# V products on 32-row groups of the array, two at a time, with U, V and the low-rank values held twice

## The chip, the cores and the metric

The kernel is one program on one NeuronCore of a Trainium2 chip. The metric is device time in microseconds (us) for one launch, and smaller is better. Three timed runs of the kernel before gave 225.97, 226.92 and 228.09 us; their median is 226.92. A separate execution was recorded by the hardware profiler, and every row of the trace quoted below is from that one. Its own device time is 224.48 us, and its span, from the first to the last instruction, is 222.7 us.

Engines are named as in the profile: PE is the matrix engine, PEld its weight loads, DVE the vector engine, ACT the scalar engine, POOL GpSimd, SP the engine whose queue issues most of the DMAs.

## What is computed

An attention layer and a mixer, both in one launch. The reference, cut to what matters:

```python
# attention: q, k, v are (4 batches, 8 heads, 768 positions, 64)
scores = q @ k.T / sqrt(64) - slope[h] * distance
scores = where(first 8 keys or the last 96 positions, scores, -1e9)
attn = softmax(scores) @ v
x = attn, heads side by side: (4, 768, 512)

# mixer: U is (768, 32), V is (32, 768), w_ch1 (512, 2048), w_ch2 (2048, 512)
h = x.T @ U @ V                       # over the positions, rank 32
u = x + h.T
out = u + relu(u @ w_ch1) @ w_ch2
```

The change touches only `h`: the product with U, which leaves 32 low-rank values per channel, and the product of these with V.

## The kernel before, in words

**Tiling.** Positions are cut into 6 blocks of 128, the 512 channels into 4 blocks of 128, which are 2 heads each. A *pair* `i` is one batch's two heads: 16 pairs, 4 per batch. Operands are fp16, sums are fp32 in the eight banks of PSUM, each 512 fp32 wide.

**A pair's steps.** Scores by matmuls with a contraction of 64, where the two heads stand on rows 0 to 63 and 64 to 127 of the array and write to different banks. In the first batch they are `st_sc` (L323, added to a bias from a matmul with all 128 rows, L316). In the other batches they are `visit` (L359): 22 matmuls in one block, 11 for each head, alternating. Then the exponential on ACT (L343 in the first batch; in the others L378, after L370 on DVE), the product with the values (`st_av`, L389 and L393), the normalisation on DVE (L406, L413), a cast to fp16 on POOL (L417).

**The low-rank part of a pair.** `st_up` (L423) for the first five pairs that need the result at once, or `st_low` (L431), its copy `st_lc` (L437, DVE) and a transpose `st_lt` (L441, PE) for the other eleven, gives the low-rank values of 128 channels. They stand on 32 partitions of PSUM, the other 96 hold zeros, because U is held in a tile 128 columns wide of which 32 are not zero. `st_tc` (L446, DVE) copies all 128 partitions to `tmp`. The product with V follows, and all of it contracts over 128 partitions of which 96 hold zeros:

- `st_M2` (L481, L486), first batch, 4 pairs: for each half of the positions one V product of 384 columns, then three matmuls that add the transposed attention into the same bank. The sum goes to `uT` by `st_ut` (ACT or DVE).
- `st_M3` (L454), other batches, 12 pairs: six V products of 128 columns, three into one bank and three into another; `st_add` (L464, L471) adds them to `x` on DVE, and a DMA transposes the sum into `uT`.
- `down_mm` (L542), first batch only: one V product of 512 columns opens the accumulation for each of the 6 blocks of output positions.

**The feed-forward part.** `up_mm` (L527) is one step `U(b, g, jt)` of four matmuls; `up_relu` (L535, ACT) takes its bank. `down_mm` (L547) has four parts of four matmuls for each block of positions in the first two batches. In the last two batches `product` (L614) takes its place, with sums on DVE (L601, L632).

**What sets the order.** The order on every engine is written by a planner inside the kernel (from L642). Every step has a planned cost, dependencies, and a count of banks; the planner keeps a clock for each engine and emits the next step that can start, and a bank is granted when the step that reads it last has its planned end. So a planned cost that changes moves steps of all engines against each other. Before 30 us of its clock it fills planned idle time of PE with `warm` matmuls (L152), whose result nothing reads. What is emitted is a fixed order; on the chip each engine runs its own queue in that order and waits by semaphores.

Of the kernel before, what the change touches and what calls it, by code (L numbers as in the profile page):

```python
# [20 lines left out]
def kernel(  # L21
# [13 lines left out]
    nc = tc.nc  # L35
# [3 lines left out]
    P = 128  # L39
# [5 lines left out]
    R = moe_U.shape[1]  # L45
# [16 lines left out]
    GT = S // 2  # L62
    NTG = GT // P
# [15 lines left out]
    banks = [psum.tile([P, 512], FP32, name=f"bank{j}") for j in range(8)]  # L79
    granted = deque()  # L80

    def bank(dtype=FP32):
        t = granted.popleft()
        return t if dtype == FP32 else t.bitcast(dtype)
# [97 lines left out]
    v16w = cst.tile([P, S], FP16, name="v16w")  # L182
    for t in (u16.rearrange("p n c -> p (n c)"), v16w):
        nc.gpsimd.memset(t.bitcast(I32), 0)
    nc.gpsimd.dma_start(u16[:, :, 0:R], moe_U.rearrange("(c p) r -> p c r", p=P))
    nc.gpsimd.dma_start(v16w[0:R], moe_V)
    ident16 = cst.tile([P, P], FP16, name="ident16")
    nc.vector.tensor_copy(ident16, ident)

# [244 lines left out]
            )  # L434

    def st_lc(i):
        nc.vector.tensor_copy(lows[i % 2][:, 0:R], tms[i][:, 0:R])  # L437

    def st_lt(i):
        back = tms[i].bitcast(FP16)[:, 4 * P:5 * P]  # L440
# [7 lines left out]
    def st_M3(i):  # L448
        b, dc = i // NP, i % NP
        for g in range(2):  # L450
            ups = bank()
            for t in range(NTG):
                n = NTG * g + t
                nc.tensor.matmul(  # L454
                    ups[:, t * P:(t + 1) * P], v16w[:, n * P:(n + 1) * P],
                    tmps[b][:, dc * P:(dc + 1) * P],
                    start=(t == 0), stop=(t == NTG - 1),
                )
            ups3[i, g] = ups

    def st_add(i, g):
        b, dc = i // NP, i % NP
# [13 lines left out]
    def st_M2(i):  # L476
        b, dc = i // NP, i % NP
        ch = slice(dc * P, (dc + 1) * P)
        for g in range(2):
            ups = bank()  # L480
            nc.tensor.matmul(  # L481
                ups[:, 0:GT], tmps[b][:, ch], v16w[:, g * GT:(g + 1) * GT],
                start=True, stop=False,
            )
            for t in range(NTG):
                nc.tensor.matmul(  # L486
                    ups[:, t * P:(t + 1) * P], x16s[b][:, dc, NTG * g + t], ident16,
                    start=False, stop=(t == NTG - 1),
                )
            ups3[i, g] = ups  # L490

    def st_ut(i, g, eng):
        b, dc = i // NP, i % NP
# [43 lines left out]
    def down_mm(b, n, part):  # L537
        g, ts = group(b, n)
        if part == 0:
            cps_t[b, n] = bank()  # L540
            if b == 0:
                nc.tensor.matmul(  # L542
                    cps_t[b, n], v16w[:, n * P:(n + 1) * P], tmps[0], start=True, stop=False,
                )
        cps, htr = cps_t[b, n], htrs[b, g]
        for jc in range(4 * part, 4 * part + 4):
            nc.tensor.matmul(  # L547
                cps, htr[:, jc, ts], w2_16[:, jc],
                start=(b > 0 and jc == 0), stop=(jc == NJC - 1),
            )  # L550
# [264 lines left out]
    def first(i):  # L815
        if i:
            casts(i)
            turns(i)
        values(i)
        for c in range(3):  # L820
            sc = add(("sc", i, c), "PE", 0.85 if c < 2 else 0.7, lambda c=c: st_sc(i, c),
                     [], banks=2, at=0 if i or not c else 7.9,
                     soft=[(("tq", i), 0.4), (("tk", i), 0.4), (("ka", i), 0.6)])
            free_of[sc] = [
                add(("ex", i, c, hi), "ACT", 0.56 if c < 2 else 0.46,
                    lambda c=c, hi=hi: st_ex(i, c, hi), [("sc", i, c), ("av", i - 2, hi)])
                for hi in range(2)
            ]
        for hi in range(2):
            a = add(("av", i, hi), "PE", 0.33, lambda hi=hi: st_av(i, hi),  # L830
                    [("ex", i, c, hi) for c in range(3)] + [("va", i), ("vp", i)], banks=1)
            free_of[a] = [add(("n", i, hi), "DVE", 0.75, lambda hi=hi: st_norm(i, hi), [("av", i, hi)])]
            if i < NP - 1:
                add(("x16", i, hi), "POOL", 0.52, lambda hi=hi: st_x16(i, hi), [("n", i, hi)])
            else:
                steps["x16", i, hi] = steps["n", i, hi]
        u = add(("up", i), "PE", 0.34, lambda: st_up(i), [("x16", i, 0), ("x16", i, 1)], banks=1)
        free_of[u] = [add(("tc", i), "DVE", 0.29, lambda: st_tc(i), [("up", i)])]
        m = add(("m2", i), "PE", 0.66, lambda: st_M2(i), [("tc", i)], banks=2)
        free_of[m] = [  # L840
            add(("ut", i, g), (("ACT", 0.48), ("DVE", 0.55)), 0,
                lambda e, g=g: st_ut(i, g, e), [("m2", i)])
            for g in range(2)
        ]

    def pair(i):
        b = i // NP
        if i < NTP:
            casts(i)
            turns(i)  # L850
        else:
            casts(i)
            add(("tp", i), "SP", 2.5, lambda: turn(i),
                [("cq", i, 0), ("cq", i, 1), ("visit", i - 2)], move=0.4, soft=[(("xt", NPE - 1), 3.0)] * (i == NPE + 1)).tail = 1.0
            add(("ka", i), "DVE", 0.7, lambda: st_K(i, nc.vector), [("tp", i)])
        values(i)
        v = add(("visit", i), "PE", 0.81, lambda: visit(i),
                [("tq", i), ("tk", i), ("ka", i), ("tp", i), ("m2", NP - 1)] + [("m3", NPE - 1)] * (i == NPE), banks=6, at=pace(i))
        got = {}
        for hi in range(2):  # L860
            for c in range(3):
                got[c, hi] = add(
                    ("s", i, hi, c), "DVE", 0.63 if c < 2 else 0.47,
                    lambda hi=hi, c=c: st_S(i, hi, c),
                    [("visit", i), ("e", i - 1, hi), ("table",)],
                )
                got[c, hi].rank = 3 * hi + c
            add(("e", i, hi), "ACT", 1.38, lambda hi=hi: st_E(i, hi),
                [("s", i, hi, c) for c in range(3)] + [("av", i - 2, hi)])
        free_of[v] = [got[c, hi] for c in range(3) for hi in range(2)]  # L870
        for hi in range(2):
            def norm(hi=hi):
                lazy_batch(b)
                st_norm(i, hi)

            a = add(("av", i, hi), "PE", 0.33, lambda hi=hi: st_av(i, hi),
                    [("e", i, hi), ("va", i), ("vp", i)], banks=1)
            free_of[a] = [add(("n", i, hi), "DVE", 0.75, norm, [("av", i, hi)])]
            add(("x16", i, hi), "POOL", 0.52, lambda hi=hi: st_x16(i, hi), [("n", i, hi)])
        if i == NPE - 1:  # L880
            u = add(("up", i), "PE", 0.34, lambda: st_up(i), [("x16", i, 0), ("x16", i, 1)], banks=1)
            free_of[u] = [add(("tc", i), "DVE", 0.29, lambda: st_tc(i), [("up", i)])]
        else:
            u = add(("up", i), "PE", 0.19, lambda: st_low(i), [("x16", i, 0), ("x16", i, 1)], banks=1)
            lc = add(("lc", i), "DVE", 0.2, lambda: st_lc(i), [("up", i), ("lt", i - 2)])
            add(("lt", i), "PE", 0.06, lambda: st_lt(i), [("lc", i)])
            free_of[u] = [add(("tc", i), "DVE", 0.29, lambda: st_tc(i), [("lt", i)])]
            free_of[u][0].first = lc
        m = add(("m3", i), "PE", 0.34, lambda: st_M3(i), [("tc", i)], banks=2)
        free_of[m] = [  # L890
            add(("add", i, g), "DVE", 0.55, lambda g=g: st_add(i, g), [
                ("m3", i), ("half", i, 0), ("half", i, 1)], lazy=0.6 if i == NPE - 1 else 0)
            for g in range(2)
        ]
        if i == NPE - 1:
            halves = [("half", i, g) for g in range(2)]
            for g in range(2):
                add(halves[g], "DVE", 0.55, lambda g=g: st_add16(i, g), [("m3", i)])
            add(("xt", i), "SP", 1.2, lambda: st_X(i), halves + [("read", b - 2)], move=0.3)
            return  # L900
        add(("cx", i), "POOL", 0.84, lambda: st_C(i), [("add", i, 0), ("add", i, 1)])
        add(("xt", i), "SP", 1.2, lambda: st_X(i), [("cx", i), ("read", b - 2)], move=0.3)
# [5 lines left out]
    for i in range(NPE, NPAIR):  # L908
        for n in (("lq", i, 0), ("lq", i, 1), ("lv", i)):
            load(n)  # L910
    for i in range(NP):
        first(i)
    xo = add(("xo",), "DVE", 1.15, st_xo, [("tc", NP - 1)])
    free_of[steps["av", NP - 1, 0]] = free_of[steps["av", NP - 1, 1]] = [xo]
    add(("table",), "POOL", 1.9, finish_table, [("m2", NP - 1)])
# [218 lines left out]
```

## Time and profile before

| | before |
|---|---|
| timed runs, median | 226.92 us |
| timed runs, lowest and highest | 225.97 and 228.09 us |
| profiled execution, own time | 224.48 us |
| profiled execution, span | 222.7 us |
| granted TensorE clock, mean | 1.000 |
| PE busy | 217.5 us, 98% of the span |
| DVE, ACT, POOL busy | 155.1, 114.3, 82.9 us |
| DMA traffic | 35.70 MB, 160 GB/s |

Busy time is summed over an engine's instructions, with overlaps counted once. In a timeline a row is one instruction, or several alike: start, time from the first one's start to the last one's end, engine, line, operation, tiles written and read, shapes, count, and in brackets the idle time ahead of it and what ended that. Matmuls are pipelined: a row of one matmul of 128 columns lasts 0.22 us, but the next one can start 0.056 us after it. Where PE is full the distance between starts is therefore what a matmul costs, and not its duration.

### The profile page before, as it was taken

To read this page: it belongs to the slowest core of one execution; us is meant where nothing else is said; L and a number is where in the kernel's file an instruction comes from. 1 tells how busy PE (TensorE), PEld (TensorE's weight loads), DVE (VectorE), ACT (ScalarE), POOL (GpSimd) and SP (SyncE) were. 2 spreads that over 40 slices of the span, in tenths; PEclk is the share of its full clock that TensorE was granted. 3 is DMA by queue.
4 is the path that set the end of the run, shared out by engine and by line. 5 is a ranking of instruction groups with operands and counts; after the bars stand their busy time and mean duration, and the time that the engine had idled before them with its cause. 6 is when DMAs were issued, how large, how long until landed. Compare 5 with 4: busy or idle time off the path is not lost.

```text
span 222.7 us, 5379 instructions
## 1 busy us (share of the span) xinstructions
PE 217.5 (98%) x2147; PEld 143.9 (65%) x2147; DVE 155.1 (70%) x351; ACT 114.3 (51%) x201; POOL 82.9 (37%) x124
## 2 busy tenths in 40 slices
PE   7999999999999999999999999999999999999994
PEld 3655876666555555665565555546988666688883
DVE  5768739576779587898978799696976602284662
ACT  5778576986464008791387041968233344444100
POOL 6646795605535632186445807223200000000000
PEclk9999999999999999999999999999999999999999
DMA  6999999999789997999799999410210400200204
GB/s 197 325 314 190 315 239 256 211 197 249 152 229 199 246 209 180 248 241 163 195 255 164 223 181 238 109 37 3 35 35 3 188 0 3 94 0 7 90 24 168
DMA packets 88872, 35.70 MB, mean 160 GB/s; under 512 B 78320, under 2 KB 85520, under 8 KB 88848
## 3 DMA queue, kind: packets, MB, share of 16 engines
q1 hardware_dynamic: 84320, 31.07, 60.1%
q0 software_dynamic: 4528, 4.29, 11.9%
q8 instruction: 17, 0.28, 0.5%
q14 instruction: 7, 0.06, 0.1%
HBM read 27.46 MB, written 6.29 MB: 152 GB/s over the span
## 4 chain that ended last, share of the span: by engine, by line
PE 88%; DMA 5%; DVE 3%; POOL 1%; ACT 1%; issue 1%; SPq 0%; POOLq 0%
PE bank L527 36%; PE bank L614 16%; PE bank L547 15%; PE bank L359 3%; PE bank L393 3%; PE bank L234 2%; PE bank L316 2%; DMA uT<-x 2%; PE bank L389 2%; PE bank L323 2%; DMA kst<-in_k_dram 2%; PE bank L454 2%; DMA qst<-in_q_dram 1%; PE bank L152 1%; DVE q L109 1%; PE bank L431 1%
## 5 line engine op out<-in xcount | busy, mean ns | idle before, releaser
L527 PE MATMUL bank<-uT,w 128*128 128x384 f16 (+2 forms) x512 | 92.7, 326 | 0.1
L535 ACT ACTIVATE htr<-bank 128x384 f16<-128x384 f32 (+2 forms) x128 | 60.2, 492 | 56.8 <-PE bank L527 47.5
L527 PEld LDWEIGHTS <-w 128*128 128x128 f16 x512 | 48.0, 98 | 27.9 <-issue 0.3
L378 ACT ACTIVATE ep<-sp 128x1408 f16<-128x1408 f32 x24 | 32.9, 1372 | 25.9 <-DVE sp L370 25.9
L547 PE MATMUL bank<-w,htr 128*128 128x512 f16 x192 | 46.1, 379 | 0.0
L370 DVE SCALAR_TENSOR_TENSOR sp<-bank,relcat 128x512 f32<-128x512 f32 (+1 forms) x72 | 41.4, 636 | 5.0 <-PE bank L359 4.8
L417 POOL CAST x<-x_sb 128x384 f16<-128x384 f32 x30 | 17.3, 579 | 36.2 <-DVE x_sb L413 36.2
L547 PEld LDWEIGHTS <-htr 128*128 128x128 f16 x192 | 17.4, 97 | 17.8
L127 POOL CAST v<-vst 128x768 f16<-128x768 f32 x16 | 14.2, 884 | 9.2 <-DMA vst<-in_v_dram 7.9
L413 DVE TENSOR_TENSOR x_sb<-bank,rcp 128x384 f32<-128x384 f32 x30 | 16.7, 557 | 1.0
L509 POOL CAST x<-x_sb 128x768 f16<-128x768 f32 x11 | 9.2, 837 | 20.9 <-DVE x_sb L464 15.3
L393 PE MATMUL bank<-v,ep 128*128 128x65 f16 x192 | 15.3, 193 | 0.2 <-ACT htr L535 0.2
L614 PEld LDWEIGHTS <-htr 128*128 128x128 f16 x144 | 14.0, 98 | 2.3
L393 PEld LDWEIGHTS <-ep 128*128 128x128 f16 x192 | 13.5, 98 | 2.3
L464 DVE TENSOR_TENSOR x_sb<-bank,x_sb 128x384 f32<-128x384 f32 x24 | 12.4, 549 | 3.2 <-PE bank L454 2.4
L389 PE MATMUL bank<-vA,ep 128*128 128x65 f16 x160 | 13.6, 194 | 0.0
L343 ACT ACTIVATE ep<-bank 128x512 f16<-128x512 f32 (+1 forms) x24 | 11.7, 576 | 2.1 <-PE bank L323 1.2
L406 DVE RECIPROCAL rcp<-bank 128x6 f32<-128x6 f32 x32 | 6.1, 189 | 9.1 <-PE bank L393 6.9
L614 PE MATMUL bank<-w,htr 128*128 128x256 f16 x96 | 12.1, 273 | 0.0
L389 PEld LDWEIGHTS <-ep 128*128 128x128 f16 x160 | 10.9, 97 | 1.8 <-issue 0.2
L284 POOL COPY vA<-v 128x650 f16<-128x650 f16 x16 | 11.7, 731 | 0.9
L632 DVE TENSOR_TENSOR osb<-bank,x_sb 128x256 f32<-128x256 f32 x12 | 5.1, 421 | 9.7 <-PE bank L614 9.7
(110 smaller groups left out, 295.0 us busy)
## 6 DMA issues: line engine op xcount, KB each, us to landing
qst<-in_q_dram SPq DMA_DIRECT2D x16, 384.0 KB, 5.6
kst<-in_k_dram SPq DMA_DIRECT2D x16, 384.0 KB, 5.7
vst<-in_v_dram SPq DMA_DIRECT2D x16, 384.0 KB, 5.8
out_dram<-osb SPq DMA_DIRECT2D x17, 256.0 KB, 2.5
w<-in_moe_w_ch_dram POOLq DMA_DIRECT2D x6, 512.0 KB, 10.0
out_dram<-vst SPq DMA_DIRECT2D x5, 256.0 KB, 2.0
w<-in_moe_w_ch_dram POOLq DMA_DIRECT2D x1, 1024.0 KB, 10.7
out_dram<-osb SPq DMA_DIRECT2D x2, 128.0 KB, 1.8
```

The source lines that it names most:

```text
L127: nc.gpsimd.tensor_copy(vt.rearrange("p n h d -> p h n d")[:, :, :, 0:D], vsts.pop(i).rearrange("p (h n) d -> p h n d", h=2),)
L370: nc.vector.scalar_tensor_tensor(out=sps[i, hi][:, c0:c0 + tot], in0=raw.pop((i, hi, c))[:, 0:tot], scalar=qk_scale / slope[2 * (i % NP) + ...
L378: nc.scalar.activation(ep, sps.pop((i, hi)), AF.Exp, scale=slope[2 * (i % NP) + hi])
L389: nc.tensor.matmul(ob[:, qi], ep[:, OF[qi - 1]:OF[qi - 1] + P], vA[:, qi - 1, hi], start=True, stop=False,)
L393: nc.tensor.matmul(ob[:, qi], ep[:, DG[qi]:DG[qi] + P], vt[:, qi, hi], start=(qi == 0), stop=True,)
L413: nc.vector.tensor_tensor(xo, ob[:, :, 0:D], rb, ALU.mult)
L417: nc.gpsimd.tensor_copy(x16, xo)
L464: nc.vector.tensor_tensor(dst, ups3.pop((i, g))[:, 0:GT].rearrange("p (t d) -> p t d", t=NTG), dst, ALU.add)
L527: nc.tensor.matmul(hps[:, 0:cols], w1_16[:, dc, jt * P:(jt + 1) * P], uTs[b][:, dc, c0:c0 + cols], start=(dc == 0), stop=(dc == NDC - 1),)
L535: nc.scalar.activation(htrs[b, g][:, jt], hps_t.pop((b, g, jt))[:, 0:TG[b][g] * P], AF.Relu)
L547: nc.tensor.matmul(cps, htr[:, jc, ts], w2_16[:, jc], start=(b > 0 and jc == 0), stop=(jc == NJC - 1),)
L614: nc.tensor.matmul(accs[b, n, acc], x[:, c], y[:, c], start=(fresh and c == 0), stop=(c == HC - 1), skip_group_check=not fresh,)
```

## The change

U, V and the low-rank values are held a second time, 64 partitions (for U, 64 columns) further on. V gets its second copy by one DVE copy (`second_v`), U by one POOL copy (`second_u`); `st_lc` writes its 32 columns at two places. With this `st_up` and `st_lt` leave the low-rank values on partitions 0 to 31 and 64 to 95, and `st_tc` copies them as before.

The V products then contract over 32 partitions instead of 128. In `st_M3` the products of the two halves of the positions alternate between partitions 0 to 31 and 64 to 95, each half into a bank of its own. In `st_M2` the two products of 384 columns stand next to each other, ahead of the six additions. In `down_mm` the single product of each block reads partitions 0 to 31. The planned cost of `st_M2` goes from 0.66 to 0.52 and that of `st_M3` from 0.34 to 0.19.

```diff
+    RG = (slice(0, R), slice(P // 2, P // 2 + R))
+
+    def second_v():
+        nc.vector.tensor_copy(v16w[RG[1]], v16w[RG[0]])
+
+    def second_u():
+        nc.gpsimd.tensor_copy(u16[:, :, RG[1]], u16[:, :, RG[0]])
...
     def st_lc(i):
-        nc.vector.tensor_copy(lows[i % 2][:, 0:R], tms[i][:, 0:R])
+        nc.vector.tensor_copy(
+            lows[i % 2].rearrange("p (a c) -> p a c", a=2)[:, :, 0:R],
+            tms[i][:, 0:R].unsqueeze(1).broadcast_to((P, 2, R)),
+        )
...
     def st_M3(i):
         b, dc = i // NP, i % NP
         for g in range(2):
-            ups = bank()
-            for t in range(NTG):
+            ups3[i, g] = bank()
+        for t in range(NTG):
+            for g in range(2):
                 n = NTG * g + t
                 nc.tensor.matmul(
-                    ups[:, t * P:(t + 1) * P], v16w[:, n * P:(n + 1) * P],
-                    tmps[b][:, dc * P:(dc + 1) * P],
+                    ups3[i, g][:, t * P:(t + 1) * P], v16w[RG[g], n * P:(n + 1) * P],
+                    tmps[b][RG[g], dc * P:(dc + 1) * P],
                     start=(t == 0), stop=(t == NTG - 1),
                 )
-            ups3[i, g] = ups
...
     def st_M2(i):
...
         for g in range(2):
-            ups = bank()
+            ups3[i, g] = bank()
             nc.tensor.matmul(
-                ups[:, 0:GT], tmps[b][:, ch], v16w[:, g * GT:(g + 1) * GT],
+                ups3[i, g][:, 0:GT], tmps[b][RG[g], ch], v16w[RG[g], g * GT:(g + 1) * GT],
                 start=True, stop=False,
             )
+        for g in range(2):
             for t in range(NTG):
                 nc.tensor.matmul(
-                    ups[:, t * P:(t + 1) * P], x16s[b][:, dc, NTG * g + t], ident16,
+                    ups3[i, g][:, t * P:(t + 1) * P], x16s[b][:, dc, NTG * g + t], ident16,
                     start=False, stop=(t == NTG - 1),
                 )
-            ups3[i, g] = ups
...
                 nc.tensor.matmul(
-                    cps_t[b, n], v16w[:, n * P:(n + 1) * P], tmps[0], start=True, stop=False,
+                    cps_t[b, n], v16w[RG[0], n * P:(n + 1) * P], tmps[0][RG[0]], start=True, stop=False,
                 )
...
-        m = add(("m2", i), "PE", 0.66, lambda: st_M2(i), [("tc", i)], banks=2)
+        m = add(("m2", i), "PE", 0.52, lambda: st_M2(i), [("tc", i)], banks=2)
...
-        m = add(("m3", i), "PE", 0.34, lambda: st_M3(i), [("tc", i)], banks=2)
+        m = add(("m3", i), "PE", 0.19, lambda: st_M3(i), [("tc", i)], banks=2)
...
+    add(("v2",), "DVE", 0.35, second_v, at=13.5)
+    add(("u2",), "POOL", 0.35, second_u, at=12)
     for i in range(NP):
         first(i)
+        steps["up", i].deps += [("v2",), ("u2",)]
```

The number of matmuls that compute something stays the same on every line. The order changes: `second_v` stands on DVE between the first L288 and the next L109, `second_u` on POOL between the first L284 and the next L127; eight more `warm` matmuls are emitted between the first `st_M2` and the first `up_mm` (9 in place of 7 in one group, 11 in place of 5 in another); and from there on dozens of steps of PE stand earlier or later than before, with the DVE, ACT, POOL and SP steps that belong to them. No step is added or dropped otherwise.

## The prediction

> **What bounds the kernel now.** The page's first part comes first, then the waits of PE, then the busy time of the long middle stretch.
>
> ```profile
> PE 217.5 (98%) x2147; PEld 143.9 (65%) x2147; DVE 155.1 (70%) x351; ACT 114.3 (51%) x201; POOL 82.9 (37%) x124
> ```
>
> ```profile
> PE bank L152 <- DVE x L147: 1.2, 1, 1.2
> PE bank L234 <- DVE q L109: 0.3, 1, 0.3
> PE bank L393 <- ACT htr L535: 0.2, 1, 0.2
> ```
>
> ```profile
> 31.00:165.00 134.00, 133.73 (x1320) 1.00 0.90 180
> ```
>
> PE is busy for 98% of the span, and all that it is known to have waited for comes to 1.7 us, of which 1.5 lies in the opening. From 31 to 165 us, where every `st_M3` and every `down_mm` of the first batch lies, 133.73 of 134.00 us are busy at full clock (the 1.00). So from 31 us on a matmul less or more on PE is its own time less or more at the end, whatever the other engines do. But busy is not the same as working: a matmul's row covers 0.2 us and the next one starts long before it ends, so a pause between two matmuls hides under the rows. The price of an edit is therefore read from starts in the timeline.
>
> **The V products now.** The group gives the count for `st_M3`, the timeline one such step and the matmul group behind it; then one `down_mm` product and the matmuls after it; then the last half of the last `st_M2` with what follows.
>
> ```profile
> L454 PE MATMUL bank<-tmp,v16w 128*128 128x128 f16 x72 | 6.0, 219 | 0.0
> ```
>
> ```profile
> 51.35 0.50 PE L454 MATMUL bank<-tmp,v16w 128*128 128x128 f16 x6
> 51.69 0.81 PE L527 MATMUL bank<-uT,w 128*128 128x384 f16 x4
> ```
>
> ```profile
> 79.04 0.38 PE L542 MATMUL bank<-tmp,v16w 128*128 128x512 f16 x1
> 79.25 1.89 PE L547 MATMUL bank<-w,htr 128*128 128x512 f16 x8
> ```
>
> ```profile
> 28.82 0.33 PE L481 MATMUL bank<-v16w,tmp 128*128 128x384 f16 x1
> 28.98 0.33 PE L486 MATMUL bank<-ident,x 128*128 128x128 f16 x3
> 29.15 0.33 PE L152 MATMUL bank<-x 128*128 128x128 f16 x3
> 29.32 0.50 PE L234 MATMUL bank<-ident,q 128*128 128x128 f16 x6
> 29.66 0.44 PE L152 MATMUL bank<-x 128*128 128x128 f16 x5
> 29.93 0.33 PE L527 MATMUL bank<-uT,w 128*128 128x384 f16 x1
> ```
>
> Six products of 128 columns take 51.69 - 51.35 = 0.34 us, 0.056 each. One of 512 columns takes 0.21, one of 384 takes 0.16. They stand gapless among their neighbours, since all use 128 rows.
>
> **What a product on part of the rows costs.** The trace of before has no matmul with a contraction of 32. It has 24 blocks with 64, paired on two row groups and two banks as the new products will be: 12 visits and 12 score steps. One visit in the timeline, with the full-height matmuls on both sides, and then the weight loads at its start:
>
> ```profile
> 34.98 0.65 PE L527 MATMUL bank<-uT,w 128*128 128x384 f16 x3
> 35.56 0.23 PE L359 MATMUL bank<-qT,kT 64*128 64x128 f16 x2
> 35.63 0.22 PE L359 MATMUL bank<-qT,kA 64*128 64x128 f16 x2
> ...
> 36.13 0.22 PE L359 MATMUL bank<-qT,kT 64*128 64x128 f16 x2
> 36.28 0.82 PE L527 MATMUL bank<-uT,w 128*128 128x384 f16 x4
> ```
>
> ```profile
> 35.56 0.10 PEld L359 LDWEIGHTS <-kT 64*128 64x128 f16 x2 [0.32 <-issue]
> ```
>
> Each row of the visit is a pair. From the second pair to the eleventh are nine steps in 36.13 - 35.63 = 0.50 us, 0.056 a pair: two matmuls for the price of one. That is the gain that the change is after. Its price stands at the edges. Three matmuls of 384 columns from 34.98 on are through at 34.98 + 3 x 0.16 = 35.46 or 35.47, but the visit starts at 35.56, 0.09 later; its weight load starts in the same hundredth, after 0.32 us in which PEld stood idle, while elsewhere a load runs ahead of its matmul. On the way out the last pair is through at 36.13 + 0.056 = 36.19, and the next matmul starts at 36.28, again 0.09 late. The first pair takes 0.07 in place of 0.056, and the four matmuls behind take 0.82 in place of 0.81. So going from full height to a row group and back costs 0.09 + 0.09 + 0.02 = 0.20 us, with nothing named as the cause but the change of height. I take this for 32 rows too, as the nearest row; the bounds are 0 (nothing here shows that 32 rows must wait as 64 do) and 0.30.
>
> The Trainium skill, page "TensorEngine Tiling (Array Packing)", section Key Properties, says that changing the tiling mode, not just the tile, drains the engine. The trace agrees with 0.09 us on each side, and the page gives no price.
>
> **Part by part, on PE.**
>
> - `st_M3`, 12 times: before 0.34. After, three pairs at 0.056 and one way in and out: 0.17 + 0.20 = 0.37 to 0.38. Plus 0.04 each, 0.5 in all.
> - `st_M2`, 4 times: the two products of 0.16 become one pair of 0.16, plus 0.20; the six additions stay. Plus 0.04 each, 0.15 in all.
> - `down_mm` of the first batch, 6 times: the single product of 0.21 has no partner and gains nothing, but now changes the height: plus 0.20 each, 1.2 in all. This is the largest term.
> - Twice, in the new order, such a product follows a visit directly: one change of height (0.09) in place of a way out and a way in (0.18). Minus 0.2.
> - Eight more `warm` matmuls at 0.056 (29.66 to 29.93 holds five): plus 0.45. They lie ahead of the first `up_mm`. Today that starts as the last warm one is through (29.66 + 5 x 0.056 = 29.94), and PE's own queue sets it. What else it needs is the last copy out of `st_M2`:
>
> ```profile
> 29.35 0.56 DVE L109 CAST uT<-bank 128x384 f16<-128x384 f32 x1 [0.30 <-PE bank L486]
> ```
>
> It ends at 29.91 and moves by the 0.15 of `st_M2` at most, to 30.06, while PE arrives at 29.93 + 0.15 + 0.45 = 30.53. So both terms count in full.
>
> Sum on PE: 0.5 + 0.15 + 1.2 - 0.2 + 0.45 = **plus 2.1 us**.
>
> **Off PE.** The second copies stand in holes of their engines, and wait for the loads of U and V:
>
> ```profile
> 5.86 1.04 POOL L185 DMA_DIRECT2D u<-in_moe_U_dram  x1
> 6.89 0.53 POOL L186 DMA_DIRECT2D v16w<-in_moe_V_dram  x1
> ...
> 13.70 0.84 POOL L127 CAST v<-vst 128x768 f16<-128x768 f32 x1 [2.38 <-DMA vst<-in_v_dram]
> ```
>
> ```profile
> u<-in_moe_U_dram POOLq DMA_DIRECT2D x1, 48.0 KB, 5.3
> v16w<-in_moe_V_dram POOLq DMA_DIRECT2D x1, 48.0 KB, 4.5
> ```
>
> ```profile
> 14.40 0.96 DVE L109 COPY kT<-bank 128x768 f16<-128x768 f16 x1 [1.38 <-PE bank L234]
> ```
>
> U lands at 5.86 + 5.3 = 11.2 and V at 11.4. POOL is idle for 2.38 us up to 13.70, waiting for a DMA; a copy no larger than that cast (0.84) fits in. DVE is idle for 1.38 us up to 14.40, waiting for PE; a copy of at most 0.96 fits. Behind them queue the value cast of POOL and the kT copy of DVE, for which PE waits; with the cover gone it is 0.4 to 0.9 us at a place where PE still has idle time filled by `warm`. I take 0. The wider `st_lc`:
>
> ```profile
> L437 DVE CAST low<-bank 128x32 f16<-128x32 f32 x11 | 2.0, 184 | 2.4 <-PE bank L431 2.4
> ```
>
> Twice the output cannot take more than twice 184 ns, so 11 x 0.18 = 2 us of a DVE that is 70% busy, none of it where PE waits; 0.
>
> **What the new order moves.** Three places. First, the value product `st_av` of the fifth pair (its second head) now stands right behind the next pair's visit, with three `up_mm` steps less ahead of it. Today's rows there, PE and then ACT:
>
> ```profile
> 43.97 2.12 PE L527 MATMUL bank<-uT,w 128*128 128x384 f16 x12
> ```
>
> ```profile
> 42.70 0.49 ACT L535 ACTIVATE htr<-bank 128x384 f16<-128x384 f32 x1 [0.16 <-PE bank L527]
> 43.35 0.49 ACT L535 ACTIVATE htr<-bank 128x384 f16<-128x384 f32 x1 [0.16 <-PE bank L527]
> 43.74 1.37 ACT L378 ACTIVATE ep<-sp 128x1408 f16<-128x1408 f32 x1
> 45.01 0.96 ACT L535 ACTIVATE htr<-bank 128x384 f16<-128x384 f32 x2
> ```
>
> The visit ends at 43.97 and three steps (12 matmuls, some 1.95 us) cover the exponential, 43.74 to 45.11. In the new order one more `up_mm` (0.65) stands ahead of the visit, which then ends at 44.62, and the exponential stands behind the ReLU of 42.70: 43.1 to 44.45. But the visit holds six banks and the last two `up_mm` hold the others, and their ReLUs queue behind the exponential: the first is done at about 44.9. PE waits 0.3.
>
> Second and third, the two waits that are there already:
>
> ```profile
> 83.53 1.20 PE L527 MATMUL bank<-uT,w 128*128 128x384 f16 x5
> ```
>
> ```profile
> 88.66 0.22 PE L359 MATMUL bank<-qT,kT 64*128 64x128 f16 x2
> 89.08 0.19 PE L393 MATMUL bank<-v,ep 128*128 128x65 f16 x1 [0.20 <-ACT htr L535]
> ```
>
> Five matmuls of 384 columns take 4 x 0.16 + 0.33 = 0.97; the row has 1.20, so 0.23 is a wait, for the transposed sum of the second batch's last pair. One more `down_mm` part now stands in between (0.87, four times 0.216), so that wait goes. The other, 89.08 - 88.66 - 0.15 = 0.27, follows from ACT after a visit, and PE that comes 0.23 earlier may lose it there again. I take minus 0.1 for the two.
>
> **The sum.** 2.1 + 0.3 - 0.1 = plus 2.3 us. The profiled execution goes from 224.48 to 226.8 (its span from 222.7 to 225.0). The median of the runs is 226.92, 2.4 above the profiled one, and the difference is carried over: **229.2**, plus 1.0%. About 1% is what a measurement of this kernel can tell from no change; the forecast stands on that line.
>
> **The rivals.**
>
> *R1: a row group of 32 waits for nothing, or for less* (the other side). Place: the edges of the 22 blocks. Without the price `st_M3` saves 12 x 0.17 = 2.0 and `st_M2` 4 x 0.16 = 0.65, `down_mm` loses nothing, the warm ones still cost 0.45: minus 2.2, with the order's 0.2 minus 2.0, 224.9. The sum turns where a round trip costs less than 0.10, half of what a visit pays. For it: the price is seen at 64 rows alone. Against: it is seen at all 24 blocks, in both directions, with the weight load idle. The Trainium skill's page "TensorE: Matmul & The Clock Gate", section Measured speedup vs the span model, has a pack of row tiles take one matmul's time and 4 ns for each further tile, with no term for going in and out; by that rule it is R1, and inside a visit the trace agrees (0.056 a pair).
>
> *R2: the two products of a pair run one after the other at 32 rows*, so the change does not do what it says. `st_M3` is then 0.34 + 0.20, plus 12 x 0.21 = 2.5; `st_M2` plus 4 x 0.20 = 0.8; the rest as above: 2.5 + 0.8 + 1.2 - 0.2 + 0.45 + 0.2 = plus 5.0, 231.9. Against it: the visits, which pair in the same way.
>
> *R3: the new order makes PE wait at more places* like the first above, say four at 0.3: plus 1.2 on the forecast, 230.4. For it: dozens of steps moved. Against: the planned costs (0.19 and 0.52) are lower than what I expect on PE, so PE comes later than planned and the others have had their time.
>
> **How the numbers follow.** Forecast 0.76, its own range 227.6 to 230.7 (the price of a round trip between 0.15 and 0.25, which is 1.1 us either way over 22 blocks, and 0.4 for waits). R1 0.11, R2 0.07, R3 0.06. Range 225.6 to 231.4: it takes in half of R1 and leaves out R2. One percent is 2.27 us. Slower by more: half of the forecast, R2 and R3, 0.51. Faster by more than 1% (below 224.65) only in half of R1: 0.05. Within: 0.44.
>
> **What would show it.** In the timeline after, a `st_M3` block in rows of two at a distance of 0.056 to 0.07, a start 0.09 late on both sides, and 0.37 from its first neighbour to the next; idle PEld ahead of it; the `down_mm` product 0.20 dearer than the 0.21 of now. The first `up_mm` at 30.5. If `st_M3` takes 0.17 to 0.2 and no weight load idles, it is R1; rows of one at 0.056 are R2. Waits of PE of over 1 us after 31 us would mean R3. The prediction is wrong if 32 rows have a price of their own, or if the moved steps open waits that I have not found.

## The result, and the profile after

The changed kernel is slower, as forecast. Its median is 228.32 us over 22 runs (227.24 to 230.58), that of the kernel before 226.16 us over 22 runs (224.68 to 228.09). The ratio is 1.0106, with a 95% interval from 1.0082 to 1.0130: plus 2.4 us, between 1.9 and 2.9. The forecast was plus 2.3 us, 229.2 on the median known then.

| | before | after |
|---|---|---|
| profiled execution, own time | 224.48 us | 227.99 us |
| profiled execution, span | 222.7 us | 225.7 us |
| PE busy | 217.5 us, 98% | 219.9 us, 97% |
| granted clock | 1.000 | 1.000 |

The lines of the functions touched now stand 7 to 11 lines further down: `st_M3` is L465, `st_M2` L491 and L497, the `down_mm` product L552, the matmuls behind it L557, `up_mm` L537, the visits L366. The first part of the page and the waits of PE, after:

```profile
PE 219.9 (97%) x2155; PEld 140.8 (62%) x2155; DVE 157.4 (70%) x351; ACT 114.6 (51%) x201; POOL 84.6 (37%) x126
```

```profile
PE bank L152 <- DVE x L147: 1.2, 1, 1.2
PE bank L451 <- DVE low L444: 0.6, 1, 0.6
PE bank L400 <- ACT htr L545: 0.4, 2, 0.2
PE bank L366 <- DVE kA L259: 0.4, 2, 0.2
```

PE has 2.4 us more that count as busy, and 1.4 us of waits behind the opening where before had 0.2 (the first row is the opening's, in both). One `st_M3` in the timeline, with its neighbours, and the weight loads of the same place:

```profile
51.38 0.81 PE L537 MATMUL bank<-uT,w 128*128 128x384 f16 x4
52.13 0.34 PE L465 MATMUL bank<-tmp,v16w 32*128 32x128 f16 x6
52.40 0.82 PE L537 MATMUL bank<-uT,w 128*128 128x384 f16 x4
```

```profile
52.12 0.17 PEld L465 LDWEIGHTS <-v16w 32*128 32x128 f16 x6 [0.32 <-DVE tmp L456]
52.40 0.11 PEld L537 LDWEIGHTS <-w 128*128 128x128 f16 x2
```

The copy that the first of these rows names, on DVE:

```profile
51.58 0.22 DVE L456 COPY tmp<-bank 128x128 f16<-128x128 f16 x1 [0.42 <-PE bank L451]
```

Four matmuls of 384 columns from 51.38 on are through at 51.38 + 4 x 0.162 = 52.03; the next full-height matmul starts at 52.40. So the step costs 0.37 us, where it cost 0.34. Inside, the pairs do what they should: from the first start to the last matmul's end the six take 0.34, where six in a row took 0.50. Of the 0.37, 0.10 passes before the first pair, and the weight load waits for it, after 0.32 us of idle. It does not wait for the copy that the row names: that ended at 51.80, 0.32 us earlier, and the load of the visit in the prediction, where no copy is named, idled for the same 0.32. What the two places share is the change of height.

One `down_mm` product, then one that follows a visit directly:

```profile
80.81 0.39 PE L552 MATMUL bank<-tmp,v16w 32*128 32x512 f16 x1
81.13 0.60 PE L557 MATMUL bank<-w,htr 128*128 128x512 f16 x2
```

```profile
59.84 0.22 PE L366 MATMUL bank<-qT,kT 64*128 64x128 f16 x2
60.00 0.38 PE L552 MATMUL bank<-tmp,v16w 32*128 32x512 f16 x1
60.31 1.04 PE L557 MATMUL bank<-w,htr 128*128 128x512 f16 x4
```

From the product to the next matmul it is 81.13 - 80.81 = 0.32, where it was 0.21: the way out costs 0.10. Behind the visit the product starts 0.16 after the last pair, and not 0.056: from 64 rows to 32 is a change like the others, 0.10.

**Where the time went.** A measure that does not depend on how soon the inputs land is the stretch of PE from the first `up_mm` to the first matmul of the last product. Its two rows, in the timeline of before and of after:

```profile
29.93 2.28 PE L527 MATMUL bank<-uT,w 128*128 128x384 f16 x13
...
218.41 1.04 PE L614 MATMUL bank<-w,kst 128*128 128x256 f16 x8
```

```profile
29.98 2.11 PE L537 MATMUL bank<-uT,w 128*128 128x384 f16 x12
...
221.59 1.04 PE L624 MATMUL bank<-w,kst 128*128 128x256 f16 x8
```

Before it is 218.41 - 29.93 = 188.48 us, after 221.59 - 29.98 = 191.61: plus 3.1. The span grew by 3.0 us (222.7 to 225.7), so all that these two profiles differ by lies there. The stretch is called S in what follows; how much of its growth is work and how much is wait, the experiments have to tell.

### The profile page after: what moved, and what is told of

Read it like the earlier page. It is cut to its first block, busy times and chain, and to the rows that moved or that the text cites. A ratio compares the mean times of both kernels' runs of the same rounds, so it can differ in the third digit from the quotient of the medians.

```text
span 225.7 us, 5410 instructions
## 1 busy us (share of the span) xinstructions
PE 219.9 (97%) x2155; PEld 140.8 (62%) x2155; DVE 157.4 (70%) x351; ACT 114.6 (51%) x201; POOL 84.6 (37%) x126
## 4 chain that ended last, share of the span: by engine, by line
PE 81%; DMA 9%; DVE 5%; SPq 2%; issue 1%; ACT 1%; POOL 1%; DVEq 0%; POOLq 0%
PE bank L537 28%; PE bank L624 16%; PE bank L557 15%; DMA kst<-in_k_dram 6%; PE bank L152 4%; DMA kT<-k 3%; PE bank L366 2%; PE bank L241 2%; PE bank L323 2%; PE bank L400 2%; PE bank L330 2%; PE bank L396 2%; DVE sp L377 2%; PE bank L465 1%; DVE kA L258 1%
## 5 line engine op out<-in xcount | busy, mean ns | idle before, releaser
L537 PE MATMUL bank<-uT,w 128*128 128x384 f16 (+2 forms) x512 | 93.2, 326 | 0.0
L537 PEld LDWEIGHTS <-w 128*128 128x128 f16 x512 | 47.6, 98 | 28.0
L557 PE MATMUL bank<-w,htr 128*128 128x512 f16 x192 | 45.9, 380 | 0.0
L424 POOL CAST x<-x_sb 128x384 f16<-128x384 f32 x30 | 18.0, 603 | 45.0 <-DVE x_sb L420 38.5
L557 PEld LDWEIGHTS <-htr 128*128 128x128 f16 x192 | 16.8, 97 | 18.6 <-issue 1.4
L127 POOL CAST v<-vst 128x768 f16<-128x768 f32 x16 | 13.7, 853 | 9.9 <-DMA vst<-in_v_dram 9.9
L519 POOL CAST x<-x_sb 128x768 f16<-128x768 f32 x11 | 9.9, 898 | 16.7 <-DVE x_sb L474 16.5
L624 PEld LDWEIGHTS <-htr 128*128 128x128 f16 x144 | 14.1, 98 | 2.3
L642 DVE TENSOR_TENSOR vst<-bank,x_sb 128x256 f32<-128x256 f32 x12 | 5.1, 425 | 8.9 <-PE bank L624 8.9
```

The lines of the kernel that those rows point to most:

```text
L127: nc.gpsimd.tensor_copy(vt.rearrange("p n h d -> p h n d")[:, :, :, 0:D], vsts.pop(i).rearrange("p (h n) d -> p h n d", h=2),)
L424: nc.gpsimd.tensor_copy(x16, xo)
L537: nc.tensor.matmul(hps[:, 0:cols], w1_16[:, dc, jt * P:(jt + 1) * P], uTs[b][:, dc, c0:c0 + cols], start=(dc == 0), stop=(dc == NDC - 1),)
L557: nc.tensor.matmul(cps, htr[:, jc, ts], w2_16[:, jc], start=(b > 0 and jc == 0), stop=(jc == NJC - 1),)
L624: nc.tensor.matmul(accs[b, n, acc], x[:, c], y[:, c], start=(fresh and c == 0), stop=(c == HC - 1), skip_group_check=not fresh,)
```

## The experiments

**Two theories.** T is that of the prediction: each way into a block on part of the rows and out of it costs PE 0.20 us, pairs give back 0.17 us for each `st_M3`, and the new order adds its own waits and eight warm matmuls. O is its rival: the loss comes from the steps that moved, and the price of the blocks hides in waits that would have been there. (That the price is none at all, R1, and that the pairs do not run at once, R2, the trace above has already answered.)

### The change in the order of before

```diff
-        m = add(("m2", i), "PE", 0.52, lambda: st_M2(i), [("tc", i)], banks=2)
+        m = add(("m2", i), "PE", 0.66, lambda: st_M2(i), [("tc", i)], banks=2)
-        m = add(("m3", i), "PE", 0.19, lambda: st_M3(i), [("tc", i)], banks=2)
+        m = add(("m3", i), "PE", 0.34, lambda: st_M3(i), [("tc", i)], banks=2)
```

> The change with the planned costs of before (0.66 and 0.34), so that every engine keeps the order of before, apart from the V products themselves and the two second copies. Theory T (each way into and out of a 32-row block costs about 0.2 us of PE, the new order adds its waits on top): 12 x 0.04 + 4 x 0.04 + 6 x 0.20 - 0.2 (one st_M3 stands directly ahead of a down_mm product) = plus 1.6 us over the kernel before, and no PE wait over 0.1 us after 31 us beyond the two of before; ratio about 1.007. Theory O (the moved steps cost the time and the price of the blocks is hidden in waits that would have been there): within 0.3 us of the kernel before.

Ratio 1.0046 (1.0015 to 1.0076), plus 1.0 us; S is 220.40 - 30.41 = 189.99, plus 1.5. Because T's 1.6 and the timing were some way apart, it was timed again:

> The change in the order of before, timed once more: its trace has 1.5 us more from the first up_mm to the last matmul and 0.15 before it, its first timing gave 1.0 us (0.3 to 1.7). By chance: plus 1.6 (0.7%); hidden in waits of the timed runs: plus 1.0 or less.

Ratio 1.0063 (1.0035 to 1.0091), plus 1.4; S 189.98. With the order of before, the change still costs 1.5 us of PE. O expected 0.3 at most. One wait that T did not have is in both profiles, 0.17 us at 109.88 in the first (by the distance of starts); the wait of 0.23 ahead of the second batch's first `up_mm`, which before has, is gone from both.

### The order of the change, without its products

```diff
-        nc.vector.tensor_copy(v16w[RG[1]], v16w[RG[0]])
+        nc.vector.tensor_copy(v16w[RG[1]], v16w[R:2 * R])
...
-                    ups3[i, g][:, t * P:(t + 1) * P], v16w[RG[g], n * P:(n + 1) * P],
-                    tmps[b][RG[g], dc * P:(dc + 1) * P],
+                    ups3[i, g][:, t * P:(t + 1) * P], v16w[:, n * P:(n + 1) * P],
+                    tmps[b][:, dc * P:(dc + 1) * P],
```

(and the same in `st_M2` and `down_mm`)

> The order of the changed kernel, instruction by instruction, but every V product contracts over all 128 partitions; the second copy of V is filled with zeros, so the result is the same. T: no 32-row blocks, so only the order is left: eight warm matmuls (0.45 us) and the waits that the order opens, which the changed kernel's profile has at 1.5 us more than before; PE is faster here and may wait more or less: plus 0.5 to 1.5 us over the kernel before. O: all of the loss, plus 2.4 us.

Ratio 1.0057 (1.0030 to 1.0084), plus 1.3; S is 219.60 - 30.72 = 188.88, plus 0.4. The waits of PE in this run:

```profile
PE bank L152 <- DVE x L147: 1.2, 1, 1.2
PE bank L400 <- ACT htr L545: 0.4, 2, 0.2
PE bank L366 <- DVE kA L259: 0.2, 1, 0.2
```

The order alone costs 0.4 us behind the first `up_mm`. The timing, 0.7 to 1.9 us by its interval, leaves 0.3 to 1.5 for the rest; the 0.45 of the eight warm matmuls has room in it, but is not shown by it. So the order costs something and is not the whole loss: in S it is 0.4 of the changed kernel's 1.9 (its second profile, below).

### The largest term taken out

```diff
-                    cps_t[b, n], v16w[RG[0], n * P:(n + 1) * P], tmps[0][RG[0]], start=True, stop=False,
+                    cps_t[b, n], v16w[:, n * P:(n + 1) * P], tmps[0], start=True, stop=False,
```

> The changed kernel, but the product of down_mm in the first batch reads all 128 partitions again, so it adds h twice in that batch; the order is that of the changed kernel. T: five of the six products lose a round trip of their own or the half of one: 1.0 us less than the changed kernel, so plus 1.3 to 1.5 over the kernel before (some of it may come back as waits). O: no difference from the changed kernel, plus 2.4.

Ratio 1.0082 (1.0051 to 1.0113), plus 1.9, and S is 220.35 - 30.88 = 189.47, plus 1.0. Against the changed kernel's S of 190.41 (its second profile, below) that is 0.94 less; T expected 1.0. The timing alone, 0.5 us under the changed kernel with intervals that overlap, would not settle it.

### The price by itself

```diff
-                    cps_t[b, n], v16w[:, n * P:(n + 1) * P], tmps[0], start=True, stop=False,
+                    cps_t[b, n], v16w[0:R, n * P:(n + 1) * P], tmps[0][0:R], start=True, stop=False,
```

> The kernel before, but the product of down_mm in the first batch contracts over partitions 0 to 31 alone (the other 96 hold zeros); no second copies, the order is that of before. This is the disputed price by itself: T: six round trips at 0.19 to 0.20 = plus 1.15 us, ratio about 1.005, and in the timeline 0.316 us from that product to the next matmul in place of 0.216. O: 0.

S is 219.90 - 30.21 = 189.69: plus 1.2, as T has it. The product in the timeline:

```profile
53.70 0.39 PE L542 MATMUL bank<-tmp,v16w 32*128 32x512 f16 x1
54.02 1.25 PE L547 MATMUL bank<-w,htr 128*128 128x512 f16 x5
```

0.32 us to the next matmul, as expected. But the timing gave 1.0018 (0.9991 to 1.0045), plus 0.4 us and just short of T's 1.005. So it was timed again, and a kernel with three times the price was made.

> The kernel before with the product of down_mm on 32 partitions, timed once more: its trace has 1.2 us more from the first up_mm to the last matmul, its first timing gave 0.4 us (minus 0.2 to 1.0). If the first timing was off by chance, plus 1.2 (0.5%); if timed runs of before hold waits that the profiled ones do not, and the price hides in them, plus 0.4 again (0.2%).

Ratio 1.0039 (1.0014 to 1.0063), plus 0.9; S 189.68.

```diff
-                    ups[:, t * P:(t + 1) * P], v16w[:, n * P:(n + 1) * P],
-                    tmps[b][:, dc * P:(dc + 1) * P],
+                    ups[:, t * P:(t + 1) * P], v16w[0:R, n * P:(n + 1) * P],
+                    tmps[b][0:R, dc * P:(dc + 1) * P],
```

(beside the edit of `down_mm` above)

> The kernel before, with the order of before, but the products of st_M3 (12 steps) and of down_mm in the first batch (6) contract over partitions 0 to 31, one after the other, no second copies and no pairs. The price alone, three times that of the run with down_mm: T: 17 round trips (one st_M3 stands directly ahead of a down_mm product) at 0.195 = plus 3.3 us over the kernel before, ratio about 1.0146, and no more waits. O: within 0.5 us of the kernel before.

Ratio 1.0109 (1.0067 to 1.0151), plus 2.5; S is 223.15 - 31.36 = 191.79, plus 3.3. The price is there, in an order that did not move at all, and grows with the number of blocks; O's 0 is out. All three timings, though, lie below their traces, by 0.3 to 0.8 us. Each but the first has the trace's figure inside its interval, so chance can do it; that timed runs of before hold some wait in which a part of the price hides was not shown and not excluded. One thing on record speaks for it: the two profiled executions of before took 224.48 and 224.87 us, at the low end of its timed runs (lowest 224.68, median 226.16), while the two of the changed kernel took 227.99 and 228.17, close to its median of 228.32. Two executions of each do not settle it.

### The pairs taken out

```diff
-                    ups3[i, g][:, t * P:(t + 1) * P], v16w[RG[g], n * P:(n + 1) * P],
-                    tmps[b][RG[g], dc * P:(dc + 1) * P],
+                    ups3[i, g][:, t * P:(t + 1) * P], v16w[RG[0], n * P:(n + 1) * P],
+                    tmps[b][RG[0], dc * P:(dc + 1) * P],
```

> The changed kernel, but both halves of st_M3 read partitions 0 to 31, so that no two products stand on different row groups; the order is that of the changed kernel. T: pairs are what gives the 0.17 us back, so each of the 12 steps goes from 0.37 to 0.54: plus 2.0 over the changed kernel, plus 4.0 to 4.4 over the kernel before (1.8 to 2.0%), less what waits give back. O: within 0.5 of the changed kernel.

Ratio 1.0177 (1.0131 to 1.0224), plus 4.0; S is 224.03 - 31.66 = 192.37, 1.96 more than the changed kernel's 190.41. One step:

```profile
52.68 0.81 PE L537 MATMUL bank<-uT,w 128*128 128x384 f16 x4
53.42 0.50 PE L465 MATMUL bank<-tmp,v16w 32*128 32x128 f16 x6
53.86 0.82 PE L537 MATMUL bank<-uT,w 128*128 128x384 f16 x4
```

From 52.68 + 0.65 = 53.33 to 53.86 are 0.53 us. So the pairs do give 0.16 to 0.17 us for each step, all that was hoped for; it is the edges that eat it.

### Planned costs as measured

```diff
-        m = add(("m2", i), "PE", 0.52, lambda: st_M2(i), [("tc", i)], banks=2)
+        m = add(("m2", i), "PE", 0.70, lambda: st_M2(i), [("tc", i)], banks=2)
-        m = add(("m3", i), "PE", 0.19, lambda: st_M3(i), [("tc", i)], banks=2)
+        m = add(("m3", i), "PE", 0.38, lambda: st_M3(i), [("tc", i)], banks=2)
-                Step("PE", 0.87 if b or j else 1.08, lambda j=j: down_mm(b, n, j), banks=(j == 0))
+                Step("PE", 0.87 if b or j else 1.28, lambda j=j: down_mm(b, n, j), banks=(j == 0))
```

> The changed kernel with planned costs as measured: 0.70 for st_M2, 0.38 for st_M3, 1.28 for the first part of down_mm in the first batch. The order is then a third one. T: 21 round trips, no more warm matmuls than before: plus 1.5 over the kernel before and fewer waits than the changed kernel's 2.06 us after the first up_mm, about 0.5; so 0.5 to 1 us faster than the changed kernel. O: the order decides, no forecast better than between 0 and plus 2.4.

S is 220.34 - 30.32 = 190.02, plus 1.5, as expected. The time is not: 1.0098 (1.0065 to 1.0132), plus 2.2 and no better than the changed kernel by anything that the timing can tell. The profiled execution has more behind the last matmul, too. That one starts at 221.10 of a span of 225.8 us, 4.70 before the end, where the two profiles of before have 3.54 and 3.38: the last output DMA landed 3.0 us after its issue, and in those two 1.9 and 1.7 us. With its opening (30.32) like theirs, S and this tail make its span longer; whether the timed runs have the late landing, the record does not show.

### The same pairs on 64 rows

```diff
+    HG = (slice(0, P // 2), slice(P // 2, P))
...
-                    ups3[i, g][:, t * P:(t + 1) * P], v16w[RG[g], n * P:(n + 1) * P],
-                    tmps[b][RG[g], dc * P:(dc + 1) * P],
+                    ups3[i, g][:, t * P:(t + 1) * P], v16w[HG[g], n * P:(n + 1) * P],
+                    tmps[b][HG[g], dc * P:(dc + 1) * P],
```

(and the same in `st_M2` and `down_mm`)

> The changed kernel with every V product contracting over 64 partitions (0 to 63 and 64 to 127), of which 32 hold zeros: the same pairs and the same order, the tile's height that of the visits. If the price is one of a change of height, the two products that follow a visit directly start 0.056 us after its last pair and not 0.148, and the others pay as with 32 rows: 0.2 us less than the changed kernel. If 32 rows have a price of their own, more changes than that.

Ratio 1.0111 (1.0067 to 1.0156), which the timing cannot tell from the changed kernel's; S is 221.83 - 31.58 = 190.25, 0.16 less than the changed kernel, where 0.2 was expected. The product behind the visit, timeline:

```profile
61.07 0.22 PE L367 MATMUL bank<-qT,kT 64*128 64x128 f16 x2
61.13 0.38 PE L553 MATMUL bank<-tmp,v16w 64*128 64x512 f16 x1
61.44 1.04 PE L558 MATMUL bank<-w,htr 128*128 128x512 f16 x4
```

It starts 0.06 after the last pair, where with 32 rows it started 0.16 after. The `st_M3` blocks, with full height on both sides, cost what they cost with 32. So the price belongs to a change of the tile's height, not to small tiles as such. The Trainium skill, page "TensorEngine Tiling (Array Packing)", section Key Properties, ties the drain to a change of the mode and not of the tile, and these two rows agree with it: 0.06 against 0.16 us.

### Both kernels profiled again

> The kernel before, unchanged, profiled once more. From the first up_mm on, its profile had 189.24 us up to the last matmul, of which 0.50 is waits, and the first up_mm at 29.93 us; the profiled execution took 224.48 us, 1.5 less than the median of all runs of before by now. If the opening and the wait ahead of the second batch's first up_mm depend on when DMAs land, both theories expect the work from the first up_mm on to stay within 0.5 us of 189.2, and the start of the first up_mm to be up to 1 us later.

S is 218.95 - 30.43 = 188.52, against 188.48; the first `up_mm` starts at 30.43, against 29.93. S repeats to a few hundredths; the opening does not.

> The changed kernel, unchanged, profiled once more. Its first profile had 2.06 us of waits after the first up_mm (0.80 and 0.37 at places where three other runs with the same order have at most 0.2). If these two belong to that one execution, the waits are now 0.9 us and the work from the first up_mm to the last matmul is 191.2 us in place of 192.4; if the order makes them, they are there again.

Its waits, and the two rows of S:

```profile
PE bank L152 <- DVE x L147: 1.2, 1, 1.2
PE bank L400 <- ACT htr L545: 0.4, 2, 0.2
PE bank L366 <- DVE kA L259: 0.2, 1, 0.2
```

```profile
31.32 0.98 PE L537 MATMUL bank<-uT,w 128*128 128x384 f16 x5
...
221.73 1.04 PE L624 MATMUL bank<-w,kst 128*128 128x256 f16 x8
```

S is 221.73 - 31.32 = 190.41: plus 1.9 over before, and not the 3.1 of the first profile. The difference of 1.2 is two waits that the first execution had and this one lacks. The larger stood here, in DVE's timeline of the first:

```profile
96.43 0.74 DVE L258 COPY kA<-kT 128x640 f16<-128x640 f16 x1 [0.78 <-DMA kT<-k]
97.20 0.17 DVE L259 COPY kA<-kT 128x32 f16<-128x32 f16 x1
97.29 0.22 DVE L444 CAST low<-bank 128x64 f16<-128x64 f32 x1
```

A copy waited for a DMA, the cast of the low-rank values was queued behind it, and PE for the cast (the 0.6 of L451 above). It depends on when a transposing DMA lands: none of the five other profiles of this order has more than 0.1 us there. The smaller wait, 0.37, stood in the first visit, at 35.09 us, behind the DVE copy L259: the copy took 1.23 us in this execution and 0.68 in the second one, and what stretched it stays open.

No kernel of these beats the one before. The one arrangement that the 64-row run points to, each `st_M3` on 64 rows right beside a visit, where the change of height is paid already, was not tried: the visit holds six banks and the products two, which is all eight, and an open `down_mm` or `up_mm` holds one of them.

## Why the prediction was right, step by step

**The price of a change of height.** Taken from the visits, 0.20 a round trip, for tiles of 32 rows. Right: 0.10 in and 0.10 out in the rows above, the same with 32 rows as with 64, and the change from 64 to 32 costs one of them. The bounds of 0 and 0.30 were not needed.

**`st_M3`.** Said 0.37 to 0.38 in place of 0.34; measured 0.37. **`st_M2`.** Said 0.36 for the pair with its edges. The last one of the first profile:

```profile
28.25 0.34 PE L491 MATMUL bank<-v16w,tmp 32*128 32x384 f16 x2
28.52 0.51 PE L497 MATMUL bank<-ident,x 128*128 128x128 f16 x6
```

0.27 to the first addition and some 0.10 ahead of it: 0.36. **`down_mm`.** Said plus 1.2 in all; alone, in the order of before, S grew by 1.2 twice; in the new order two of the six stand right behind a visit, as said. The largest term, and it is one on which the planned costs were left as they were.

**The sum on PE behind the first `up_mm`.** 2.1 less the 0.15 of `st_M2` and 0.45 of warm ones, which lie ahead of it, is 1.5. S grew by 1.9, of which waits are 0.4 by the next points: 1.5.

**The opening.** Said plus 0.6, first `up_mm` at 30.5. Not settled by single profiles: 29.98 and 31.32 after, 29.93 and 30.43 before. Over all profiles, six with the new order start it at 31.0 on average (29.98 to 31.66) and eight with other orders at 30.6 (29.93 to 31.36). The sign agrees, the size is lost in the spread. PE's own part of the term is there: 86 `warm` matmuls (L152) in place of 78, and 0.04 for each `st_M2`. The spread has at least two sources in the traces. PE's waits for the casts of q and k, in the view of waits, are none in the first profile of after and 1.9 us in the run with `st_M3` and `down_mm` on 32 rows in the order of before. And PE starts its first matmuls at about twice the usual distance, for a time that differs: the same seven `warm` matmuls of 128 columns take 0.39 us from 5.32 on in the first profile of after (0.056 each) and 0.75 from 5.45 on in the second (0.107 each).

The second copies found their holes, as said:

```profile
L190 DVE COPY v16w<-v16w 32x768 f16<-32x768 f16 x1 | 0.4, 351 | 0.0
L193 POOL COPY u<-u 128x192 f16<-128x192 f16 x1 | 0.6, 580 | 1.0 <-DMA u<-in_moe_U_dram 1.0
```

POOL waited 1.0 us for U's load and then again for the next load of v, so the copy delayed nothing there.

**The order's waits.** Three places were named. At the fifth pair's value product 0.3 was said: the product starts 45.31 - 44.89 = 0.42 after the visit's last pair, 0.27 later than a way out takes (0.15):

```profile
44.89 0.22 PE L366 MATMUL bank<-qT,kT 64*128 64x128 f16 x2
45.31 0.19 PE L400 MATMUL bank<-v,ep 128*128 128x65 f16 x1 [0.20 <-ACT htr L545]
```

The wait ahead of the second batch's first `up_mm` was to go, and is gone:

```profile
85.42 1.30 PE L537 MATMUL bank<-uT,w 128*128 128x384 f16 x7
```

Seven matmuls in 6 x 0.16 + 0.33 = 1.30, without a pause. The third stayed at 0.27 and did not take in what the second gave up:

```profile
90.32 0.22 PE L366 MATMUL bank<-qT,kT 64*128 64x128 f16 x2
90.74 0.19 PE L400 MATMUL bank<-v,ep 128*128 128x65 f16 x1 [0.20 <-ACT htr L545]
```

What the step missed is a fourth place. In a later visit PE waits 0.35 for a copy that now stands late on DVE, in every profile of this order:

```profile
128.74 0.22 PE L366 MATMUL bank<-qT,kT 64*128 64x128 f16 x2
129.14 0.23 PE L366 MATMUL bank<-qT,kA 64*128 64x128 f16 x2 [0.18 <-DVE kA L259]
```

So the order costs plus 0.4 in waits (0.27 + 0.35 - 0.23) where 0.2 was said: the term was mis-sized by what was not looked for. The sign given for R3, over 1 us of waits behind 31 us, turned up in the first profile (0.50 before, 2.06 after, by the distances of starts) and not in the second (0.89); one profile would have misled. That a slower PE finds the others ready was no safe argument against R3: a wait for a DMA two steps up the chain came through once, and the 0.35 of the fourth place every time.

**The rivals.** R1 fell: the edges are paid at 32 rows. R2 fell: taking the pairs out costs 2.0 more (its sum has 12 x 0.21 where its own 0.34 + 0.20 gives 0.20 a step; the 0.1 us decides nothing). Of R3 one place stands in every profile of this order, 0.35 us and not 1.2. The measured ratio and the forecast's, 1.0101, lie within 0.1% of each other, both at the line of 1% on whose sides the forecast laid a half each; on which side it came out is luck, and part of the agreement too, since the waits were 0.2 us more than said and the opening stayed unsettled.

## What to carry to other kernels

Before small contractions are packed onto row groups, count the changes of the tile's height: each block that stands alone among full-height matmuls costs some 0.2 us here, which three pairs of 128 columns (0.17 us gained) do not pay, and for which a lone product gains nothing. The price of a form that a kernel did not use yet could here be read at the edges of one that it does use, from the distance of starts and not from busy time. And where a planner orders by costs, a wrong one moves other steps: here the new order holds 0.4 us of waits in S. Costs as measured took these away (S plus 1.5 in place of 1.9), but that the kernel got faster by it was not shown.

## What the runs showed that was not expected

A tile with half of its rows zero is cheaper than the exact one if its neighbours have that height: behind a visit the 64-row product starts after 0.06 us, the 32-row product after 0.16. And two profiles of the same kernel can differ by 1.2 us in the waits of the bound engine, 0.8 of it behind one transposing DMA that landed late and 0.4 behind one stretched copy, while without such waits the same stretch of 190 us repeats to 0.04 us (188.48 and 188.52 before; 189.69 and 189.68, 189.99 and 189.98 for the two kernels that were run twice).
